# The tail's threshold search counted in steps, its capacity test on ScalarE, its final table of 16 columns

## The chip, the core and the metric

One core of a Trainium2 chip runs the whole program. The metric is the device time of one execution in microseconds (us), the median over several runs. The engines named below are TensorE (PE; its weight loads are listed as PEld), VectorE (DVE), ScalarE (ACT), GpSimd (POOL) and SyncE (SP). Each works through its own instructions in the order of the program; they run beside each other and meet at semaphores.

## What is computed

Three stages follow each other. An attention without softmax makes 12288 rows of 256: `out = u * (relu(z z^T / S)^2 v)`. Then come two layers of eight experts (256 to 1024 to 256). What matters here is how the first layer gives tokens to experts:

```python
logits = x @ w_gate
order = np.argsort(-logits.flatten())
for idx in order:
    tok, e = idx // E, idx % E
    if assigned[tok] >= 0 or counts[e] >= cap:
        continue
    assigned[tok] = e
    counts[e] += 1
```

So the pairs of token and expert are taken from the highest logit down, each expert takes at most `cap` = 1536 tokens, and a token whose expert is full waits for its next best. The second layer routes each token to its best expert and keeps the first 384 of each expert.

## The kernel before

**Order of the stages.** Attention goes over 24 chunks of 512 queries, and the routing of the first layer begins in its shadow. With a threshold `t0`, found from the first three quarters of the tokens (`prep`, L681), every token whose best logit is above `t0` goes to its best expert: the "head". All others, at most 19 x 128, are scattered into a small table in DRAM (`tt`) and are the "tail", together with the last 512 tokens. `tail` (L784) places them.

**The tail's search.** A phase (L833 to L899; nine of them) masks the full experts (LM), takes each remaining token's best logit V and its one-hot TH, and lowers a threshold `hi` as far as no expert gets more than its remaining capacity `kcol`. The threshold is found in three rounds of 32 candidates. A round compares V with the 32 candidates (G, 128 x 23 x 32, L856 or L858), counts per expert with 23 small matmuls (L866, the "capacity test"), compares the counts with `kcol` (gO, L868, VectorE), spreads the result to all partitions with one matmul (L871, the "broadcast") and sums the steps that were not over (gX, L874). After the three rounds NW marks the tokens that are placed (L878), one matmul counts them (L890), and the experts that are full now are masked in the next phase. The size of the next phase's steps is the whole remaining range if a further expert got full, else the finest step (L880 to L887, L839). After the ninth phase the tokens get positions (L904 to L928), and a table of 48 columns, six blocks of 128 places for each of the eight experts, is made by 23 matmuls (L939, `table` at L561, matmul L587). Its columns 4 and 5 of each six are used by the tail.

**Units.** The first layer runs 16 units (`seq`, L1514): eight of width 432, one per expert, for head tokens from the first 40 x 128 places, and then eight of width 256 for tail tokens. A unit has eight blocks f = 0 to 7; a block is six matmuls of layer 1 (L1013), and six of layer 2 (L1163) for the block two before. ScalarE makes the relu hH (L1021) and VectorE the rest hL (L1023). The next weights are loaded by SyncE and split by ScalarE (pH, L220, 128x1024) and VectorE (pL, L225). In blocks 2 to 5 the previous unit's output gets its logits (L1114) and is scattered (L1118); from block 6 on small VectorE steps for the second routing trickle out (L1134 to L1141).

**What sets the order.** `Follow` (L54) puts the steps of `tail` between the matmuls. The program keeps a plan's clock for TensorE, `tp`, and one for VectorE, `td`. At a side point (after each but the last matmul of a group of six, and twice at a block's end) the next step of the tail is issued if `tp` has reached `ready`. Each `yield` of the tail gives costs: a part for TensorE, `pe` (0.25 if not given), one for VectorE, an `extra` and a `lead`:

```python
m.tp += pe
m.dve(d, 0.2)            # td = max(td, tp + 0.2) + d
self.ready = m.td + 0.15 - lead
m.td += extra
```

Other work moves the two clocks too: a matmul adds w/2400 to `tp`, a logit group 0.46 and a turned block of 128 tokens 0.1; hL and the low part of turned tokens add 0.5 to `td`, pL 1.2 (blocks 1, 3, 5, 7), the trickled steps 0.2, 0.35, 0.8 and 0.25, at most one at each of the slow side points (four in a block).

**The forced point.** A unit's gather goes out at block 6 two units before (L1188). Unit 8 needs the tail's table, so its gather waits until block 3 of unit 7, and `late` (L1527) first calls `finish`, which issues all that is left of the tail's steps, one after another.

**Other lines.** `consts` (L135) makes constants early. `row` (L1339) in `ffn2` scales output rows into `orow`; `fin` (L1170) uses `yT` in the first layer. If a check fails, a flag starts `general` (L1473), which does both layers again in a slower way.

Of the kernel before, what the change touches and what calls it, by code (L numbers as in the profile page):

```python
# [53 lines left out]
class Follow:  # L54
# [24 lines left out]
class Moe:  # L79
# [55 lines left out]
    def consts(self, wg1, wg2):  # L135
# [3 lines left out]
        self.idr = c.tile([128, 128], FR, name="idr")  # L139
        nc.scalar.activation(self.idr, self.idf, AF.Copy)  # L140
# [643 lines left out]
    def tail(self, rows):  # L784
# [9 lines left out]
        w3 = c.tile([128, 3], F32, name="w3")  # L794
        for i in range(3):
            nc.vector.memset(w3[:, i:i + 1], float(NTH) ** -i)
# [14 lines left out]
        nc.vector.tensor_scalar(iv, tok[:, :TD], 0.5, -1e36, op0=OP.is_lt, op1=OP.mult)  # L811
# [12 lines left out]
        nc.vector.scalar_tensor_tensor(LT[:, TD:], H[:, :, None].to_broadcast([128, 4, E]), -1e36,  # L824
# [3 lines left out]
        self.diag(k8, kcol)  # L828
        nc.vector.tensor_scalar(cl0, k8, 0.5, 0.0, op0=OP.is_lt, op1=OP.add, accum_out=cc)
        hi = self.t0  # L830
        PH = E + 1
        cl, c2, NW = cl0, cc, None
        for ph in range(PH):  # L833
            LM = R.tile(sh, F32, name="LM")
            nc.vector.scalar_tensor_tensor(LM, cl[:, None, :].to_broadcast(sh), -1e30, LT, op0=OP.mult, op1=OP.add)
            s3 = R.tile([128, 3], F32, name="s3")
            if ph:

                nc.vector.scalar_tensor_tensor(s3, sd[:, 0], d, sd[:, 1], op0=OP.mult, op1=OP.add)  # L839
                cc = c2  # L840
                yield 0.0, 0.5, 0.0, 0.5
            else:
                nc.vector.tensor_scalar(s3, w3, st, None, op0=OP.mult)
            V = R.tile([128, TC], F32, name="tV")
            nc.vector.tensor_reduce(V, LM, AX.X, OP.max)
            M = R.tile([128, NTH], F32, name="gM")
            nc.vector.tensor_scalar(M, self.mrow, s3[:, 0:1], hi, op0=OP.mult, op1=OP.add)
            TH = R.tile(sh, BF, name="tTH")
            nc.vector.tensor_tensor(TH, LM, V[:, :, None].to_broadcast(sh), OP.is_equal)
            yield 0.0, 0.85 if ph else 2.0, 0.0, 0.5  # L850
            for i in range(3):
                G = R.tile([128, TC, NTH], BF, name="gG", tag="gG", bufs=1)
                Vb = V[:, :, None].to_broadcast([128, TC, NTH])
                Mb = M[:, None, :].to_broadcast([128, TC, NTH])
                if i == 0:
                    nc.vector.tensor_tensor(G, Vb, Mb, OP.is_ge)  # L856
                else:
                    nc.vector.scalar_tensor_tensor(G, Vb, sn, Mb, op0=OP.subtract, op1=OP.is_ge)  # L858
                    hi = self.plus(hi, sn)
                if i < 2:  # L860
                    M = R.tile([128, NTH], F32, name="gM")
                    nc.vector.tensor_scalar(M, self.mrow, s3[:, i + 1:i + 2], hi, op0=OP.mult, op1=OP.add)
                yield 0.25, 1.2 if i else 0.9, 0.3
                pc = self.rt()
                for j in range(TC):
                    nc.tensor.matmul(pc[:E, :NTH], TH[:, j, :], G[:, j, :], start=j == 0, stop=j == TC - 1)  # L866
                over = R.tile([E, NTH], BF, name="gO")
                nc.vector.tensor_scalar(over, pc[:E, :NTH], kcol, None, op0=OP.is_gt)  # L868
                yield 0.6, 0.2
                pa = self.rt()  # L870
                nc.tensor.matmul(pa[:, :NTH], self.ones[:E, :], over, start=True, stop=True)  # L871
                x = R.tile([128, NTH], F32, name="gX")
                sn = R.tile([128, 1], F32, name="gn")
                nc.vector.scalar_tensor_tensor(x, pa[:, :NTH], 0.5, s3[:, i:i + 1].to_broadcast([128, NTH]),  # L874
                                               op0=OP.is_lt, op1=OP.mult, accum_out=sn)
            hi = self.plus(hi, sn)
            NW = R.tile(sh, BF, name="tNW")
            nc.vector.scalar_tensor_tensor(NW, V[:, :, None].to_broadcast(sh), hi, TH, op0=OP.is_ge, op1=OP.mult)  # L878
# [727 lines left out]
```

## Time and profile before

| | |
|---|---|
| median of 3 runs | 1636.5 us (1636.49 to 1637.97) |
| profiled execution | 1636.56 us |
| its span, first to last instruction | 1634.8 us |
| mean granted TensorE clock | 0.983 of 2.4 GHz |
| busy: PE, DVE, ACT, POOL | 97%, 73%, 68%, 20% |
| attention, until about | 1106 us |
| first layer, until about | 1460 us |

The profile is of one execution. A matmul's duration covers its way through the array, and matmuls overlap, so the distance of two starts tells what one costs, and a busy share of TensorE is not a share of its peak. The granted clock is 1.00 at 2.4 GHz and 0.50 at 1.2 GHz.

### The profile page before, as it was taken

Reading aid. Unit: us, or ns where it says so; the run is one execution under the profiler, and the core shown is the slowest. Engines: PE = TensorE matmul, PEld = TensorE weight load, DVE = VectorE, ACT = ScalarE, POOL = GpSimd, SP = SyncE. Lnnn points to the kernel's source line nnn. Section 1 sums busy time; section 2 is a strip of 40 time slices with the busy share of each in tenths; the row PEclk is TensorE's granted clock in tenths of the full one; section 3 lists DMA queues with packets and bytes.
Section 4 is the critical chain, followed back from the end, with each engine's and each line's share of the span. In section 5 each row is a group of like instructions: output and inputs, shape, how many; then the busy total and the mean of one; then the engine's idle time right before and its main releaser. Section 6 shows DMA issues by size and latency. Waiting matters only on the chain.

```text
span 1634.8 us, 24914 instructions
## 1 busy us (share of the span) xinstructions
PE 1580.8 (97%) x8570; PEld 1326.7 (81%) x8570; DVE 1186.5 (73%) x2338; ACT 1116.7 (68%) x1937; POOL 333.1 (20%) x518
## 2 busy tenths in 40 slices
PE   8999999999999999999999999999999969989997
PEld 5888887888888888888887777878888759978997
DVE  6877788777778767777877877677777766775652
ACT  7877788777788877778987767884444316644552
POOL 1000000000000000000000478642333113323341
PEclk9999999999999999999999999999999969999999
DMA  6111355322335212224310112223343204644540
GB/s 136 20 27 33 68 136 133 73 70 76 72 67 130 76 46 59 59 66 86 77 33 21 28 20 45 60 80 118 101 124 103 84 19 134 189 134 124 153 129 28
DMA packets 282681, 132.44 MB, mean 81 GB/s; under 512 B 216717, under 2 KB 268173, under 8 KB 282544
## 3 DMA queue, kind: packets, MB, share of 16 engines
q1 hardware_dynamic: 269264, 106.90, 26.0%
q0 software_dynamic: 13280, 23.85, 5.0%
q8 instruction: 69, 1.13, 0.3%
q14 instruction: 68, 0.56, 0.1%
HBM read 84.61 MB, written 40.55 MB: 77 GB/s over the span
## 4 chain that ended last, share of the span: by engine, by line
PE 70%; issue 16%; DVE 7%; POOL 2%; ACT 2%; DMA 1%; SPq 1%; POOLq 0%; DVEq 0%
PE acc L397 12%; PE acc L398 12%; PE acc L399 12%; PE sc L1013 9%; PE sc L368 6%; PE sc L369 6%; PE acc L1163 5%; PE mi L1114 2%; DVE pL L225 1%; PE rt L866 1%; PE mi L336 1%; PE acc L1320 1%; PE acc L1321 1%; PE acc L1322 1%; DVE hL L1023 1%
## 5 line engine op out<-in xcount | busy, mean ns | idle before, releaser
L382 DVE TENSOR_TENSOR aL<-a,aH 128x512 fp32r<-128x512 f32 x576 | 398.6, 693 | 212.9 <-ACT a L377 157.8
L371 ACT ACTIVATE r<-sc 128x512 f32<-128x512 f32 x576 | 343.0, 595 | 186.6 <-PE sc L369 180.7
L397 PE MATMUL acc<-aH,pH 128*128 128x512 f32 x1152 | 449.7, 390 | 0.0
L398 PE MATMUL acc<-aL,pH 128*128 128x512 f32 x1152 | 449.0, 390 | 0.0
L399 PE MATMUL acc<-aH,pL 128*128 128x512 f32 x1152 | 448.5, 389 | 0.0
L379 DVE TENSOR_TENSOR a<-r 128x512 f32<-128x512 f32 x344 | 238.5, 693 | 43.0 <-ACT r L371 41.8
L397 PEld LDWEIGHTS acc<-aH,pH 128*128 128x128 f32 x1152 | 216.7, 188 | 45.6
L399 PEld LDWEIGHTS acc<-aH,pL 128*128 128x128 f32 x1152 | 216.7, 188 | 45.6
L398 PEld LDWEIGHTS acc<-aL,pH 128*128 128x128 f32 x1152 | 216.7, 188 | 45.5
L368 PE MATMUL sc<-zHL 128*128 128x512 f32 x576 | 229.8, 399 | 6.3 <-DVE zHL L280 6.0
L1021 ACT ACTIVATE hH<-sc 128x432 fp32r<-128x432 f32 (+2 forms) x192 | 90.0, 469 | 212.5 <-PE sc L1013 208.2
L369 PE MATMUL sc<-zLH,zHL 128*128 128x512 f32 x576 | 225.3, 391 | 0.2 <-DVE zLH L284 0.2
L380 ACT ACTIVATE aH<-r 128x512 fp32r<-128x512 f32 x344 | 217.8, 633 | 10.9
L347 POOL TENSOR_TENSOR lgs<-lgb 32x128 f32<-32x128 f32 x23 | 15.2, 659 | 853.2 <-DVE lgb L344 853.2
L376 ACT ACTIVATE aH<-r 128x512 fp32r<-128x512 f32 x232 | 146.7, 632 | 7.4
L1023 DVE SCALAR_TENSOR_TENSOR hL<-sc,hH 128x432 fp32r<-128x432 f32 (+2 forms) x192 | 99.3, 523 | 65.6 <-ACT hH L1021 65.4
L377 ACT ACTIVATE a<-r 128x512 f32<-128x512 f32 x232 | 142.8, 616 | 0.0
L368 PEld LDWEIGHTS sc<-zHL 128*128 128x128 f32 x576 | 108.7, 189 | 36.1 <-DVE zHL L280 7.4
L1013 PE MATMUL sc<-xTH,pH 128*128 128x384 f32 (+2 forms) x368 | 125.9, 342 | 5.9 <-DVE hL L1023 5.8
L369 PEld LDWEIGHTS sc<-zLH,zHL 128*128 128x128 f32 x576 | 108.8, 189 | 21.5 <-DVE zLH L284 0.5
L1013 PE MATMUL sc<-xTL,pH 128*128 128x384 f32 (+2 forms) x368 | 120.0, 326 | 0.0
L1013 PE MATMUL sc<-xTH,pL 128*128 128x384 f32 (+2 forms) x368 | 119.8, 326 | 0.0
(333 smaller groups left out, 2261.4 us busy)
## 6 DMA issues: line engine op xcount, KB each, us to landing
raw<-in_moe_w_dram SPq DMA_DIRECT2D x84, 512.0 KB, 3.7
raw<-in_v_dram SPq DMA_DIRECT2D x24, 512.0 KB, 4.3
uraw<-in_u_dram SPq DMA_DIRECT2D x192, 64.0 KB, 2.3
out_dram<-zt SPq DMA_DIRECT2D x24, 512.0 KB, 4.2
xb<-xT SPq DMA_DIRECT2D x14, 512.0 KB, 3.4
zr<-in_z_dram SPq DMA_DIRECT2D x96, 64.0 KB, 2.4
zLH<-zHL POOLq DMA_DIRECT2D x46, 128.0 KB, 2.3
ya<-zt SPq DMA_DIRECT2D x10, 544.0 KB, 3.5
```

What stands on the lines that cost most here:

```text
L368: nc.tensor.matmul(p, lw, zHL[b, c % QC], start=True, stop=False)
L369: nc.tensor.matmul(p, lw, zLH[c], start=False, stop=True)
L371: nc.scalar.activation(r, p, AF.Relu, scale=SCALE)
L376: nc.scalar.activation(HS[s], r, AF.Square)
L377: nc.scalar.activation(a, r, AF.Square)
L379: nc.vector.tensor_tensor(a, r, r, OP.mult)
L380: nc.scalar.activation(HS[s], r, AF.Square)
L382: nc.vector.tensor_tensor(LS[s], a, HS[s].bitcast(F32), OP.subtract)
L397: nc.tensor.matmul(accs[h], vh[sl], HS[s], start=k == 0, stop=False)
L398: nc.tensor.matmul(accs[h], vh[sl], LS[s], start=False, stop=False)
L399: nc.tensor.matmul(accs[h], vl[sl], HS[s], start=False, stop=k == KT - 1)
L1013: nc.tensor.matmul(p, a, b[:, d, :w], start=i == 0, stop=i == 5)
```

## The change

- `Follow`: a yield of five values adds the first to `tp` and sets `ready` to the last after that, without regard to `td`.
- The search counts in steps from the last threshold: U = (V - hi) / st once a phase, compared with fixed rows 1..32, and these times 1/32 and 1/1024 (`m3`); N is the steps taken so far. The per-round rows of thresholds (L847, L862) fall away.
- The capacity test is a relu with the negated capacity as bias, on ScalarE, in place of VectorE's comparison. The step to the next phase is made by three small ScalarE operations and one of VectorE.
- The search's large numbers (1e30 to 1e36) become multiples of the first step, `mk`.
- The place codes (`ti`, `jv`, `pv`), `base`, the early mask and two GpSimd fills move from behind the search to ahead of it. The ninth phase's count and the overflow test move behind the table.
- The table has 2 columns for each expert in place of 6, and `seq` takes columns 2e and 2e + 1. A further check is added after it.
- `consts` loses `idr`, which nothing reads; `row` writes the three rows of a unit into one tile that has the tag of `yT`, of one buffer, in place of three buffers.

The search and the yields (of before, lines with a minus that repeat L834 to L928 are left out; the new code follows in full as far as it has yields):

```diff
                 y = next(self.g)
+                if len(y) == 5 if isinstance(y, tuple) else False:
+
+                    m.tp += y[0]
+                    self.ready = m.tp + y[4]
+                    return
                 pe, d, extra, lead = (y + (0.0, 0.0))[:4] if isinstance(y, tuple) else (0.25, y, 0.0, 0.0)
...
+        w3, m3 = [self.onef[:, :NTH]], [self.mrow]
+        for i in (1, 2):
+            w3.append(c.tile([128, NTH], F32, name="w3%d" % i))
+            m3.append(c.tile([128, NTH], F32, name="m3%d" % i))
+            nc.vector.memset(w3[i], float(NTH) ** -i)
+            nc.vector.tensor_scalar(m3[i], self.mrow, float(NTH) ** -i, None, op0=OP.mult)
         st = R.tile([128, 1], F32, name="st")
         nc.vector.tensor_scalar(st, self.t0, self.lo0, -1.0 / NTH, op0=OP.subtract, op1=OP.mult)
+
+        mk = c.tile([128, 4], F32, name="mk")
+        for i, x in enumerate((-29, 23, 27, -28)):
+            nc.vector.tensor_scalar(mk[:, i:i + 1], st, (1 if x > 0 else -1) * 2.0 ** abs(x), None, op0=OP.mult)
+        lon = c.tile([128, 1], F32, name="lon")
+        nc.vector.tensor_scalar(lon, self.lo0, -1.0 / NTH, None, op0=OP.mult)
...
+        bc = lambda x: x[:, :, None].to_broadcast([128, TC, NTH])
+        for ph in range(PH):
+            LM = R.tile(sh, F32, name="LM", bufs=1)
+            nc.vector.scalar_tensor_tensor(LM, cl[:, None, :].to_broadcast(sh), mk[:, 1:2], LT, op0=OP.mult, op1=OP.add)
+            V = R.tile([128, TC], F32, name="tV")
+            nc.vector.tensor_reduce(V, LM, AX.X, OP.max)
+            if ph:
+                d = R.tile([128, 1], F32, name="std2")
+                nc.vector.tensor_tensor(d, c2, cc, OP.is_gt)
+                st = R.tile([128, 1], F32, name="st")
+                nc.vector.scalar_tensor_tensor(st, dd, d, fine, op0=OP.mult, op1=OP.add)
+                cc = c2
+            U = R.tile([128, TC], F32, name="tU")
+            rs = R.tile([128, 1], F32, name="trs1")
+            nc.vector.reciprocal(rs, st)
+            nc.vector.tensor_scalar(U, V, hi, rs, op0=OP.subtract, op1=OP.mult)
+            N = None
+            for i in range(3):
+                G = R.tile([128, TC, NTH], BF, name="gG", tag="gG", bufs=1)
+                Mb = m3[i][:, None, :].to_broadcast([128, TC, NTH])
+                if i == 0:
+                    nc.vector.tensor_tensor(G, bc(U), Mb, OP.is_le)
+                    TH = R.tile(sh, BF, name="tTH")
+                    nc.vector.tensor_tensor(TH, LM, V[:, :, None].to_broadcast(sh), OP.is_equal)
+                else:
+                    nc.vector.scalar_tensor_tensor(G, bc(U), N, Mb, op0=OP.subtract, op1=OP.is_le)
+                yield 0.25, 1.45 if i else 2.2
+                pc = self.rt()
+                for j in range(TC):
+                    nc.tensor.matmul(pc[:E, :NTH], TH[:, j, :], G[:, j, :], start=j == 0, stop=j == TC - 1)
+                over = R.tile([E, NTH], BF, name="gO")
+                nc.scalar.activation(over, pc[:E, :NTH], AF.Relu, bias=kcol)
+                yield 0.8, 0.0, 0.0, 0.0, 0.45
+                pa = self.rt()
+                nc.tensor.matmul(pa[:, :NTH], self.ones[:E, :], over, start=True, stop=True)
+                x = R.tile([128, NTH], F32, name="gX")
+                sn = R.tile([128, 1], F32, name="gn")
+                nc.vector.scalar_tensor_tensor(x, pa[:, :NTH], 0.5, w3[i], op0=OP.is_lt, op1=OP.mult,
+                                               accum_out=sn)
+                N = self.plus(N, sn) if i else sn
+            NW = R.tile(sh, BF, name="tNW")
+            nc.vector.scalar_tensor_tensor(NW, U[:, :, None].to_broadcast(sh), N, TH, op0=OP.is_le, op1=OP.mult)
+            if ph < PH - 1:
+                h = R.tile([128, 1], F32, name="thi")
+                nc.scalar.activation(h, N, AF.Identity, scale=st, bias=hi)
+                hi = h
+                fine = R.tile([128, 1], F32, name="fine")
+                nc.scalar.activation(fine, st, AF.Copy, scale=float(NTH) ** -3)
+                dd = R.tile([128, 1], F32, name="std")
+                nc.scalar.activation(dd, hi, AF.Abs, scale=1.0 / NTH, bias=lon)
+                nc.vector.scalar_tensor_tensor(dd, dd, -1.0, fine, op0=OP.mult, op1=OP.subtract)
+            nc.vector.scalar_tensor_tensor(LT, NW, mk[:, 0:1], LT, op0=OP.mult, op1=OP.add)
+            if ph == PH - 1:
+                break
+            yield 0.25, 1.1, 0.5
+            pn = self.rt()
+            nc.tensor.matmul(pn[:, :TC * E], self.ones, NW.rearrange("p j g -> p (j g)"), start=True, stop=True)
+            cn = R.tile([128, E], F32, name="tcn")
+            nc.vector.tensor_reduce(cn, pn[:, :TC * E].rearrange("p (j g) -> p g j", g=E), AX.X, OP.add)
+            cl = R.tile([128, E], F32, name="cl")
+            c2 = R.tile([128, 1], F32, name="cc")
+            nc.vector.scalar_tensor_tensor(cl, cn, 0.0, k8, op0=OP.add, op1=OP.is_ge, accum_out=c2)
...
+        yield 0.25, 2.0
...
+        yield 0.3, 1.3
-        yield from self.table(px, s, TC, 6 * E, jv, pv, pool=False)
+        yield from self.table(px, None, TC, 2 * E, jv, pv, pool=False, i=s)
...
-            o = self.f.tile([128, 256], F32, name="orow", bufs=3)
+            if t == 0:
+                O[n] = self.f.tile([128, 2, self.WA], F32, name="orow", tag="yT", bufs=1).rearrange("p a b -> p (a b)")
+            o = O[n][:, t * 256:(t + 1) * 256]
...
-        seq += [(e, [6 * e + 4 + t for t in range(2)], m.WB, m.TB) for e in back]
+        seq += [(e, [2 * e + t for t in range(2)], m.WB, m.TB) for e in back]
```

## Rows read from the trace of the kernel before

**Rows 1.** The page, part 1: busy time, share of span, instructions
```profile
PE 1580.8 (97%) x8570; PEld 1326.7 (81%) x8570; DVE 1186.5 (73%) x2338; ACT 1116.7 (68%) x1937; POOL 333.1 (20%) x518
```
**Rows 2.** Stretches: length, busy PE, PEld, DVE, ACT, POOL, granted clock, DMA share, GB/s
```profile
1112.00:1300.00 188.00, 184.81 (x1390) 156.97 (x1390) 144.43 (x452) 78.04 (x136) 56.01 (x82) 1.00 0.36 111
...
1310.00:1315.00 5.00, 1.55 (x47) 1.43 (x47) 3.75 (x13) 0.00 (x0) 0.00 (x0) 0.50 0.00 2
...
1330.00:1335.00 5.00, 4.94 (x22) 4.19 (x20) 2.89 (x20) 0.53 (x1) 1.00 (x1) 0.50 0.00 0
```
**Rows 3.** Timeline of PE, 1303 to 1337: start, duration (us), engine, line, operation
```profile
1303.12 0.36 PE L1163 MATMUL acc<-hH,pL 128*128 128x432 f32 x1
1303.41 0.73 PE L866 MATMUL rt<-gG,tTH 128*8 128x32 bf16 x23
...
1331.83 0.71 PE L1013 MATMUL sc<-xTH,pH 128*128 128x432 f32 x1
...
1334.13 1.11 PE L1114 MATMUL mi<-sel,yT 128*128 128x136 f32 x4
1334.88 0.72 PE L1163 MATMUL acc<-hH,pH 128*128 128x432 f32 x1
...
1336.89 0.36 PE L1013 MATMUL sc<-xTH,pH 128*128 128x432 f32 x1
```
**Rows 4.** Timeline of POOL at 1334, with idle time before and what ended it
```profile
1333.90 1.00 POOL L969 DMA_INDIRECT g<-xa,tkgb  x1 [29.47 <-DVE b L950]
```
**Rows 5.** The search: lines by source and tile (first and last start); timeline, eighth phase
```profile
L866 PE MATMUL rt<-gG,tTH x621: 176/176/189, 1125.6 to 1317.6; 128*8 128x32 bf16 x156
...
L868 DVE TENSOR_SCALAR gO<-rt,kcol x27: 237/239/240, 1126.3 to 1317.8; 8x32 bf16<-8x32 f32 x27
...
1299.21 0.73 PE L866 MATMUL rt<-gG,tTH 128*8 128x32 bf16 x23
```
**Rows 6.** Timeline of PE, a test and a broadcast between FFN matmuls
```profile
1149.81 0.35 PE L1013 MATMUL sc<-xTL,pH 128*128 128x432 f32 x1
1150.09 0.73 PE L866 MATMUL rt<-gG,tTH 128*8 128x32 bf16 x23
...
1151.05 0.36 PE L1163 MATMUL acc<-hL,pH 128*128 128x432 f32 x1
...
1151.44 0.35 PE L1163 MATMUL acc<-hH,pH 128*128 128x432 f32 x1
1151.72 0.18 PE L871 MATMUL rt<-gO,ones 8*128 8x32 bf16 x1
...
1152.14 0.36 PE L1163 MATMUL acc<-hH,pL 128*128 128x432 f32 x1
```
**Rows 7.** Chain of waits: start, us, the head's table, eight matmuls
```profile
948.23 1.46 PE tabh L587 x8
```
**Rows 8.** Waits, 1108 to 1303: engine, who for, us in total, times, longest
```profile
PEld sc L1013 <- DVE hL L1023: 4.4, 6, 1.4
...
PE sc L1013 <- DVE hL L1023: 2.2, 4, 1.1
...
DVE gO L868 <- PE rt L866: 21.6, 21, 2.9
```
**Rows 9.** ACT by form: first row 1112 to 1300, others the whole span
```profile
L220 ACT ACTIVATE pH<-raw 128x1024 fp32r<-128x1024 f32 x26 | 27.3, 1051 | 0.0
...
L1345 ACT ACTIVATE orow<-acc,gt 128x256 f32<-128x256 f32 x16 | 7.6, 472 | 3.2 <-PE acc L1322 2.2
...
L1306 ACT ACTIVATE ex<-l 128x24 f32<-128x24 f32 x8 | 1.8, 223 | 8.7 <-DVE l L1304 8.6
L279 ACT ACT_TABLE_LOAD x1 | 1.3, 1283 | 0.7 <-PEq L1587 0.7
```
**Rows 10.** Timeline of DVE and PE, a phase's head inside the stop
```profile
1309.06 0.34 DVE L892 TENSOR_REDUCE tcn<-rt 128x8 f32<-128x184 f32 x1
...
1311.80 0.78 PE L866 MATMUL rt<-gG,tTH 128*8 128x32 bf16 x23 [3.33 <-DVE gG L856]
```

More of the change, by code (lines that the diff above doesn't have):

```diff
@@ L921, in tail @@
-        base = R.tile([128, E], F32, name="tbase", bufs=1)
-        nc.vector.tensor_scalar(base, self.hc, float(self.WA), 511.0 - self.WA, op0=OP.max, op1=OP.add)
-        yield 0.7
-        p = self.rt()
-        nc.tensor.matmul(p[:, :E], self.low, tot, start=True, stop=True)
-        nc.vector.tensor_tensor(base, base, p[:, :E], OP.add)
-        nc.vector.tensor_tensor(inc, inc, base[:, :, None].to_broadcast([128, E, TC]), OP.add)
-        s = self.slot_code(inc, oh, TC)
-        yield 1.1
+        NF = self.JF * 128
@@ L937, in tail @@
         nc.vector.tensor_scalar(pv, ti[:, 2], 1.0, None, op0=OP.add)
-        yield 0.4
-        px = self.rt("tabt")
-        yield from self.table(px, s, TC, 6 * E, jv, pv, pool=False)
-        tab = c.tile([128, 2, 6 * E], F32, name="tabB")
-        nc.vector.tensor_tensor(tab.rearrange("p a h -> p (a h)"), px[:, :12 * E],
-                                self.tabH.rearrange("p a h -> p (a h)"), OP.add)
-        self.TB.update(self.tokens(tab[:, 0], tab[:, 1], 6 * E, "b", NF))
-        yield 0.7
+        hi = self.t0
@@ new lines, in tail @@
+        nc.vector.tensor_copy(tot, inc[:, :, TC - 1])
+        yield 0.25, 2.0
+        p = self.rt()
+        nc.tensor.matmul(p[:, :E], self.low, tot, start=True, stop=True)
+        nc.vector.tensor_tensor(base, base, p[:, :E], OP.add)
+        nc.vector.tensor_tensor(inc, inc, base[:, :, None].to_broadcast([128, E, TC]), OP.add)
+        nc.vector.tensor_tensor(inc, inc, oh, OP.mult)
+        s = R.tile([128, TC], I32, name="scs%d" % TC, bufs=1)
+        with nc.allow_low_precision("whole numbers"):
+            nc.vector.tensor_reduce(s, inc.rearrange("p g j -> p j g"), AX.X, OP.add)
@@ new lines, in tail @@
+        yield 0.3, 1.3
+        px = self.rt("tabt")
+        yield from self.table(px, None, TC, 2 * E, jv, pv, pool=False, i=s)
+        tab = c.tile([128, 2, 2 * E], F32, name="tabB")
+        nc.vector.tensor_tensor(tab.rearrange("p a (e h) -> p a e h", h=2),
+                                px[:, :4 * E].rearrange("p (a e h) -> p a e h", a=2, h=2),
+                                self.tabH.rearrange("p a (e h) -> p a e h", h=6)[:, :, :, 4:6], OP.add)
+        self.TB.update(self.tokens(tab[:, 0], tab[:, 1], 2 * E, "b", NF))
@@ new lines, in tail @@
+        yield 0.7
+        FIN = R.tile(sh, BF, name="FIN", bufs=1)
+        nc.vector.tensor_scalar(FIN, LT, mk[:, 3:4], None, op0=OP.is_ge)
+        pn = self.rt()
+        nc.tensor.matmul(pn[:, :TC * E], self.ones, NW.rearrange("p j g -> p (j g)"), start=True, stop=True)
+        cn = R.tile([128, E], F32, name="tcn")
+        nc.vector.tensor_reduce(cn, pn[:, :TC * E].rearrange("p (j g) -> p g j", g=E), AX.X, OP.add)
+        self.over = c.tile([128, E], F32, name="ovr")
+        nc.vector.tensor_tensor(self.over, cn, k8, OP.is_gt)
@@ L1285, in ffn2 @@
         nc, tc, E, NF = self.nc, self.tc, self.E, self.F // 128
[L1286 removed]
+        X, G, GT, ACC, O, scat = {}, {}, {}, {}, {}, []
         T = self.T2
```

121 lines of the change are left out of this document (24 added, 97 removed).

## The prediction

> **What bounds the kernel now.** The page comes first: TensorE is busy for 97% of the span [rows 1]. That is a mean over stages, so the second view is the table of stretches. From 1112 to 1300 us, in the first units of the first expert layer, TensorE has work for 184.8 of 188 us, VectorE for 144, ScalarE for 78. From 1310 to 1315 TensorE has 1.55 us of work in 5, VectorE 3.75, and the granted clock is 0.50, the lower of the two levels (1.2 GHz); it is still 0.50 when work has resumed, from 1330 to 1335 [rows 2]. So one place is not bound by TensorE. The third view, TensorE's own timeline, gives its edges: the last FFN matmul starts at 1303.12, then only the tail's matmuls run, and the next FFN matmul starts at 1331.83 [rows 3]. With 0.20 us for the last one (1151.05 to 1151.44 is two [rows 6]), the stop lasts 28.5 us. After it one block runs at the low clock: six matmuls of layer 1, one logit group (1334.13 to 1334.88), six of layer 2, until 1336.89: 5.1 us [rows 3]. At full clock twelve at 0.20 and the group at no more than its 0.75 are 3.15. The stop's whole price is 28.5 + 1.9 = 30.4 us.
>
> What it waits for: unit 8 is the first that uses tokens of the tail, and its gather is the point (L1188, `late`) where `finish` issues all that is left of the tail with nothing between. The gather goes out at 1333.90, after 29.5 us of idle GpSimd, behind the tail's last VectorE work [rows 4]. The tail's first capacity test had run at 1125.6; the first test of its eighth of nine phases, at 1299.21 [rows 5].
>
> **What the change does to the order.** A tail step goes out when the plan's clock tp reaches `ready`. These are no times but the program's own arithmetic, which sets the order. A phase's yields with nothing else on VectorE (pe + 0.2 + cost + 0.15 - lead for a step dated by VectorE) add up, before, to 0.35 + 0.7 + 1.5 + 1.8 + 1.8, three tests of 1.15, 1.5 and 1.2 = 12.3; after, to 2.8 + 2.05 + 2.05, three tests of 0.8 + 0.45, and 1.7 = 12.35. Alone, the two are equal. But all ten steps of before are dated by td, so each also stands behind whatever hL, pL and one-hot work the plan has queued; of the seven after, the three tests are dated by tp alone. Following the plan through every block puts the first tests of the phases, before, at tp 17.2, 35.7, 56.5, 79.1, 100.4, 122.7, 145.7 and 167.2: 21.4 a phase, so 0.9 of queue a step. The forced point is at 170.5, with the eighth phase's second test next, and that test is what the trace has at 1303.41 [rows 3]. For the change the same arithmetic gives 15.0, 29.4, 43.4, 59.4, 73.8, 90.0, 107.5, 121.6 and 139.5: 15.5 a phase, or 12.35 and four queues of 0.8. The table's last step is at 167.4, in unit 6, block 6; the forced point, unit 7, block 3, is at 180.9 (later, as all of the tail's own pe now counts ahead of it). `finish` then finds nothing to do, with five blocks to spare: **the stop goes whole, 30.4 us.**
>
> **What comes back.** The stop's work has to run between FFN matmuls. From 1149.81 to 1151.05 lie two ordinary intervals and one capacity test: 0.84 for the test. From 1151.44 to 1152.14 lie two and a broadcast: 0.30 [rows 6]. Five of each remained: 4.2 + 1.5. Two counts and the offset matmul: 0.7, at the broadcast's price or less. The table's 23 matmuls, now of 32 columns: at most 23/8 of 1.46 = 4.2, by the head's table of 96 columns [rows 7]; at least one test's 0.84, which also has 23 of 32 columns but weights of 8 columns. The table's weights stay 128 wide, so near the upper: 3.6. Together 10.0, and net so far 30.4 - 10.0 = **20.4 us**. Sixteen columns instead of 48, and the positions prepared ahead, also save VectorE work behind the last phase; hidden under TensorE that is worth nothing more, and without the cover it is part of the 28.5 already counted.
>
> New waits, which the trace only bounds:
> - *ScalarE's test.* The broadcast follows the test by at least three FFN matmuls in the plan (0.45), 0.6 us. The activation takes between 0.22 (128x24, constants only) and 0.47 (128x256, with a pointer); near the small one, 0.3 [rows 9], so the slack is 0.3. ScalarE works in order, and behind the test stands the next hH. Split copies pH of 1.05 fill 27.3 of 188 us, 15% [rows 9]; caught behind one, the mean rest is 0.5, of which some 0.25 passes the slack: 27 x 0.15 x 0.25 = 1.0, and as much for hH, yT and yr: 2.0. Bounds: 0, and 20 if all 27 meet a whole pH (0.75 each). The VectorE form is 0.239 but stands for 21.6 us in line until tests end [rows 5, 8], so the trace favours the move. The Trainium skill ("ScalarE: Activation LUTs", rules for kernel authors) speaks against it: relu belongs on VectorE. By its figure for an activation with a pointer bias (an estimate of 307 ns for 32 elements) the sum stays as it is; by the rule itself the move is a loss.
> - *A phase's head.* From the count's reduction to the first test is 2.74 us, 1309.06 to 1311.80, with nothing else on VectorE [rows 10]. The change drops a threshold row and adds a reciprocal and a rescaling in series: about 3.2. With 0.55 for the count and the wake-up ahead of it, 3.7. The plan allows at least 2.8 units, which are 3.2 us (153.3 units from the first test to the forced point took 177.7 us, 1.16 each), and more than three units at six of eight heads. Eight at 0.3: 2.5. Bounds 0 and 8.
> - *Phase 0*, where eight small operations now stand ahead of the search (each at most a test's 0.24): 1.5. Bounds 0 and 3.
> - *Setup's extra small operations, and unit 8's gather*, which now has two blocks to land: 0.5. Bounds 0 and 2.
> - *A phase's end.* VectorE's step update now waits for three small ScalarE operations in a row, 0.22 each, with the marking of NW as cover. Behind it stand LT and the next hL; TensorE's next tail matmul, the count, needs only NW. It goes into the next term.
> - *The other way.* TensorE waits 4.4 + 2.2 us for hL in this stretch, and VectorE stands 21.6 us in front of tests [rows 8]. That stand goes. Phases are a quarter denser, so I take 2.5 of the 6.6. Bounds: +6.6, and -6 if the density wins.
>
> The identity copy, the markers, the two fills on GpSimd (earlier now, ahead of no gather), and the second layer's rows in one shared tile: nothing; they lie under attention or TensorE, or behind scatters issued a unit earlier. No DMA moves but the gather. Were the shared tile tracked as a whole, the last unit would wait for its own scatters, a few us.
>
> Sum: 20.4 - 2.0 - 2.5 - 1.5 - 0.5 + 2.5 = 16.4. The profiled execution took 1636.56 (span 1634.8 and 1.8 around it) and the median is 1636.50; they agree. 1636.5 - 16.4 = **1620**.
>
> **Rivals.**
> - *Clean hiding.* No new wait shows and most hL waits go: 20.4 + 5 = 25.4, so 1611. For: VectorE's freed stand. Against: heads that need more than the plan allows. Chance 0.13.
> - *A wait at each step.* Heads at 0.6, tests at 0.25: 20.4 - 4.8 - 6.8 - 2 + 2.5 = 9.3, so 1627. For: ScalarE's order, denser phases. Against: ScalarE's 78 of 188 us. Chance 0.17.
> - *Still late.* If the order slipped by more than the five blocks, some 10 us of stop and the low clock would stay: 1636.5 - 18.5 + 7 + 4 = 1629. Against: the same arithmetic hits the present point exactly. Chance 0.03.
> - *Slower: ScalarE's queue ahead of every broadcast.* The broadcast stands in TensorE's in-order stream, so a late activation stops the FFN behind it. It decides once the mean wait over 27 steps passes 16.4/27 + 0.07 = 0.7 us; at 1.05, a whole split copy each time, it is 1620 + 27 x 0.98 = 1646. For: the copies are that long and often follow an hH. Against: their 15%. Table loads for Abs and Identity, 1.28 us each, two a phase, would bring it about; the profile has one load in all, though Copy, Relu, Square and Exp take turns [rows 9]. The Trainium skill (same page, table sets) says that copy, identity, relu and abs are in every set; by it no load is added. No row here shows Abs or Identity. Chance 0.05.
> - *It doesn't do what it says.* If the rescaled search ends elsewhere, the flag sends everything through the general path, both layers again, over 500 us (1112 to 1635): 2140 or more. Chance 0.01.
>
> **How the numbers follow.** Forecast 0.61, by itself 1615 to 1626. A measurement of this kernel can tell about 0.2%, 3.3 us; same is 1633.2 to 1639.8. Faster: the forecast, clean hiding, the waits less 0.02, and late less 0.01: 0.91. Same 0.03, slower 0.06. The range 1611 to 1630 leaves out the lower half of clean hiding (0.06), the upper third of the waits (0.06), half of late, and the slow cases: 0.2.
>
> **What would show it.** Right: no stretch without FFN matmuls in unit 7, granted clock 1.00 from 1112 to the end of unit 15, first tests some 18 us apart (15.5 x 1.16), the table before unit 7, and GpSimd's gather for unit 8 with no tail work ahead of it. By step: about 2 us of broadcasts waiting for ScalarE, about 4 of first tests waiting for VectorE, hL waits down. Wrong: tail matmuls alone between 1300 and 1330; over 10 us of waits for ScalarE's test; a forced gather.

## The result, and the profile after

The change made the kernel slower: 1654.35 us (median of four runs, 1652.22 to 1656.82) against 1637.24 (1636.49 to 1638.07), a ratio of 1.0105, 95% interval 1.0085 to 1.0125: 1% slower. The profiled execution took 1656.35, its span is 1654.2, with a mean granted clock of 0.989. The forecast was 1620, range 1611 to 1630.

The busy line of the page, which answers to [rows 1], shows nothing of it: TensorE at 97% in both.

```profile
PE 1609.1 (97%) x8568; PEld 1324.9 (80%) x8570; DVE 1181.4 (71%) x2266; ACT 1130.4 (68%) x1987; POOL 334.6 (20%) x518
```

TensorE has as many instructions and 28 us more of work, so single instructions became longer. The table of stretches says where. Its columns are those of [rows 2]. First a stretch of attention, before and then after:

```profile
300.00:400.00 100.00, 100.00 (x443) 82.09 (x442) 73.86 (x112) 77.93 (x132) 4.53 (x9) 1.00 0.33 79
```

```profile
300.00:400.00 100.00, 100.00 (x431) 79.68 (x430) 71.25 (x107) 75.36 (x126) 3.03 (x6) 1.00 0.30 71
...
1137.00:1325.00 188.00, 177.76 (x1423) 145.72 (x1421) 146.79 (x431) 85.01 (x176) 52.69 (x76) 0.99 0.32 101
...
1225.00:1230.00 5.00, 4.75 (x36) 3.71 (x37) 4.83 (x20) 1.64 (x3) 0.32 (x3) 0.66 0.46 118
...
1325.00:1345.00 20.00, 19.03 (x118) 16.48 (x117) 15.41 (x60) 7.23 (x13) 4.47 (x9) 1.00 0.30 95
```

In 100 us of attention, with TensorE busy throughout and the clock at 1.00, 431 matmuls start instead of 443. A block of attention is eight matmuls. TensorE's timeline shows the second of one block and the second of the next, eight distances apart, of before:

```profile
329.83 0.39 PE L369 MATMUL sc<-zLH,zHL 128*128 128x512 f32 x1
...
331.64 0.39 PE L369 MATMUL sc<-zLH,zHL 128*128 128x512 f32 x1
```

and of after:

```profile
339.95 0.40 PE L372 MATMUL sc<-zLH,zHL 128*128 128x512 f32 x1
...
341.81 0.40 PE L372 MATMUL sc<-zLH,zHL 128*128 128x512 f32 x1
```

That is 1.81 against 1.86 us for a block. Over 100 to 900 us the mean distance of one 512-column matmul from the next is 227.0 ns before and 233.2 after. Attention has 4608 of them, so the distance makes 28.6 us. Its last one starts at 1106.0 before and at 1137.2 after. I call what is left from there to the end of the span the *rest*: 528.7 us before, 517.0 after. So the rest, in which the tail lies and which the change is about, gained 11.7 us, nearly all of it in the first layer (from attention's last matmul to the layer's last one 352.2 before, 340.1 after), and attention, which it doesn't touch, lost 31.2.

In the rest, the stop of [rows 3] is gone. The table is built in unit 6, between expert matmuls; its timeline and that of GpSimd:

```profile
1328.71 0.45 PE L1186 MATMUL acc<-hH,pH 128*128 128x432 f32 x1
1329.00 0.70 PE L590 MATMUL tabt<-tR,tL 128*128 128x32 bf16 x8
1329.52 0.45 PE L1186 MATMUL acc<-hL,pH 128*128 128x432 f32 x1
...
1354.05 0.99 POOL L992 DMA_INDIRECT g<-xa,tkgb  x1 [0.30 <-issue]
```

Unit 8's first gather (1354.05) waits for nothing but the issue; in [rows 4] it came after 29.47 us behind the tail. The waits from 1137 to 1340, to be read against [rows 8]:

```profile
DVE gX L904 <- PE rt L901: 25.2, 18, 2.5
ACT gO L898 <- PE rt L896: 23.5, 19, 3.3
...
PEld sc L1036 <- DVE hL L1046: 5.3, 5, 1.9
PEld L896 <- DVE tTH L890: 4.9, 5, 1.6
...
PE sc L1036 <- DVE hL L1046: 3.4, 3, 1.5
PE rt L896 <- DVE tTH L890: 3.3, 4, 1.3
PE rt L901 <- ACT gO L898: 0.3, 1, 0.3
```

The stand in front of the tests (21.6 us on VectorE) is now ScalarE's (23.5), and broadcasts wait for it 0.3 us in all. But VectorE still stands 25.2 us in front of the broadcasts' results (gX); before, it had this wait beside that for the tests:

```profile
DVE gX L874 <- PE rt L871: 11.8, 17, 1.9
```

A row of PEld and one of PE can be the same stall, seen by the weight load and by the matmul behind it, as in these two of one wait each:

```profile
PEld sc L1036 <- DVE xTL L1011: 2.3, 1, 2.3
PE sc L1036 <- DVE xTL L1011: 1.9, 1, 1.9
```

So such rows must not be added. What a stall costs is the distance from the start of the last matmul ahead of it (here 1222.95) to the start of the next (1225.25), less an ordinary one (0.20 us, or 0.28 ahead of a test): 2.1 here. Counted so, first tests (L896) cost 3.5 us after the change, 1.4 of it in phase 0 (none before); the waits for hL went from 3.2 to 4.3, and those for xTL, the low part of the turned tokens, from 1.1 to 3.4. The stall at 1225 lies behind a phase's head, through which VectorE works before it comes to xTL, and ahead of the only part of the first layer at the lower clock (0.66 from 1225 to 1230). ScalarE's new operations by form, for [rows 9]:

```profile
L898 ACT ACTIVATE gO<-rt,kcol 8x32 bf16<-8x32 f32 x27 | 7.5, 276 | 23.9 <-PE rt L896 23.5
...
L916 ACT ACTIVATE std<-thi,lon 128x1 f32<-128x1 f32 x8 | 2.4, 295 | 0.0
...
L282 ACT ACT_TABLE_LOAD x1 | 1.3, 1283 | 0.7 <-PEq L1612 0.7
```

A test takes 276 ns (0.3 forecast), and there is still one table load. The Trainium skill ("ScalarE: Activation LUTs", table sets) has copy, identity, relu and abs in every set. This trace agrees.

### The profile page after: what moved, and what is told of

It is laid out like the page before. It is cut to its first block, busy times and chain, and to the rows that moved or that the text cites. A ratio compares the mean times of both kernels' runs of the same rounds, so it can differ in the third digit from the quotient of the medians.

```text
span 1654.2 us, 24878 instructions
## 1 busy us (share of the span) xinstructions
PE 1609.1 (97%) x8568; PEld 1324.9 (80%) x8570; DVE 1181.4 (71%) x2266; ACT 1130.4 (68%) x1987; POOL 334.6 (20%) x518
## 4 chain that ended last, share of the span: by engine, by line
PE 69%; issue 17%; DVE 8%; ACT 2%; POOL 1%; DMA 1%; SPq 1%; POOLq 0%; DVEq 0%; ACTq 0%
PE acc L401 12%; PE acc L400 12%; PE acc L402 12%; PE sc L1036 8%; PE sc L371 6%; PE sc L372 6%; PE acc L1186 4%; DVE pL L228 1%; PE mi L1137 1%; PE mi L339 1%; PE acc L1343 1%; PE acc L1345 1%; PE acc L1344 1%; DVE hL L1046 1%; PE rt L896 1%
## 5 line engine op out<-in xcount | busy, mean ns | idle before, releaser
L385 DVE TENSOR_TENSOR aL<-a,aH 128x512 fp32r<-128x512 f32 x576 | 399.3, 694 | 232.4 <-ACT a L380 185.3
L401 PE MATMUL acc<-aL,pH 128*128 128x512 f32 x1152 | 460.7, 400 | 0.0
L400 PE MATMUL acc<-aH,pH 128*128 128x512 f32 x1152 | 455.9, 396 | 0.0
L371 PE MATMUL sc<-zHL 128*128 128x512 f32 x576 | 233.4, 405 | 7.7 <-DVE zHL L283 6.9
L372 PE MATMUL sc<-zLH,zHL 128*128 128x512 f32 x576 | 229.1, 398 | 0.2 <-DVE zLH L287 0.2
L383 ACT ACTIVATE aH<-r 128x512 fp32r<-128x512 f32 x344 | 217.8, 633 | 10.9
```

The lines of the kernel that those rows point to most:

```text
L371: nc.tensor.matmul(p, lw, zHL[b, c % QC], start=True, stop=False)
L372: nc.tensor.matmul(p, lw, zLH[c], start=False, stop=True)
L383: nc.scalar.activation(HS[s], r, AF.Square)
L385: nc.vector.tensor_tensor(LS[s], a, HS[s].bitcast(F32), OP.subtract)
L400: nc.tensor.matmul(accs[h], vh[sl], HS[s], start=k == 0, stop=False)
L401: nc.tensor.matmul(accs[h], vh[sl], LS[s], start=False, stop=False)
```

## The experiments

**What the code can do to attention.** No instruction of attention differs. But the change drops `idr` (512 bytes), makes the search's and the table's tiles smaller and adds others, and attention's pool lies behind them. By the addresses in the compiled programs attention's tiles start 1184 bytes lower: at 158432 instead of 159616, with V's tiles (the weights `pH`, `pL` of the value part) at 41344 instead of 41856. My first theory was a start off a multiple of 64. Four kernels tried it, three with an unused tile in front of attention's pool (`[128, 8]` for 32 bytes, `[128, 24]` for 96; later `[128, 40]` for 160 and `[128, 104]` for 416) and one with `idr` put back:

```diff
+        pad = R.tile([128, 8], F32, name="pad", bufs=1)
+        nc.gpsimd.memset(pad, 0.0)
         t = R.tile([128, ncol], F32, name="ck0", bufs=1)
```

```diff
         make_identity(nc, self.idf)
+        self.idr = c.tile([128, 128], FR, name="idr")
+        nc.scalar.activation(self.idr, self.idf, AF.Copy)
```

The changed kernel with 32 bytes:

> The changed kernel with one unused tile of 32 bytes per partition more ahead of attention's tiles; nothing else differs, and no instruction of the tail, of attention or of the expert layers changes. Attention's tiles then start at a multiple of 64 bytes again (158464 instead of 158432), as they did in the kernel before (159616). Theory (the placement of attention's moving operands): 512-column matmuls of attention 227 ns apart, as before, instead of 231 to 235; the first expert matmul at about 1106 us instead of 1137.5; the time 1654.4 - 31 = 1623 to 1626, ratio to the kernel before 0.992 to 0.994. Rival (the new code itself, its ScalarE and VectorE work, or the chip): attention stays 31 us longer, 1652 to 1657.

The kernel before with 32 bytes:

> The kernel before with the same unused 32 bytes, which put attention's tiles at 159648, 32 above a multiple of 64. Theory (placement): the matmuls of attention 231 to 235 ns apart, first expert matmul at about 1137 us, the time 1636.5 + 31 = 1666 to 1669, with the stop in unit 7 as before. Rival (the new code): 1636 to 1638, as before.

The changed kernel with 96 bytes:

> The changed kernel with 96 unused bytes instead of 32: attention's tiles at 158528, a multiple of 64 and not of 128 (before: 159616, a multiple of 128). Theory with 64 bytes as the unit: as with 32 unused bytes, 1623 to 1626. Rival with 128 bytes as the unit: attention slow, 1652 to 1657, and the multiple of 64 of the 32-byte variant, which is also one of 128, would not have told them apart.

The changed kernel with `idr`:

> The changed kernel with the rounded copy of the identity put back where it was (512 bytes and one ScalarE copy in the first microseconds). Attention's tiles then start at 158944, still 32 above a multiple of 64, and the tiles of the expert layers and constants lie where the kernel before has them relative to the copy. Theory (placement modulo 64): still slow, 1652 to 1657. Rival (what hurt is that the copy is gone, or the 512-byte move of the constants): about 1624.

Measured: 1668.78, 1677.83, 1678.70 and 1671.98 us, where the kernel before took 1659.5 on this chip. Spacings: 232.5, 232.2, 232.5 and 233.2 ns. So 64 bytes is not it: neither of the two kernels whose start became a multiple of 64 was mended. But the second half of the theory held: 32 unused bytes slow the kernel before as well (432 starts in the stretch that had 443), with none of the new code:

```profile
300.00:400.00 100.00, 100.00 (x432) 79.97 (x431) 71.56 (x107) 75.98 (x128) 4.52 (x9) 1.00 0.31 73
```

**Distance instead of address.** In the kernel before, the addresses of attention's tiles and of V's both leave a remainder of 384 when divided by 512; in the others they don't. The second four, with controls, since this chip's times were not the first one's. One edit,

```diff
+        nc.gpsimd.memset(c.tile([128, 8], F32, name="padc"), 0.0)
         self.idr = c.tile([128, 128], FR, name="idr")
```

moves V's and attention's tiles together (in the kernel before).

The kernel before, unchanged:

> The kernel before, unchanged, with its trace, as the control of this job: the chip of the last job gave 1653 to 1664 for it, against 1636 to 1638 on the first. If the 512-column matmuls' spacing of attention belongs to the kernel and its addresses, it is 227 ns here too, whatever the chip, and a longer time lies in stalls elsewhere (the one of 5 us at 1036 us which the last job's runs show). If it belongs to the chip, the spacing moves with the time: at 1660 it would be 227 + 20/4.6 = 231.

The changed kernel, unchanged:

> The changed kernel, unchanged, as the second control: spacing 231 to 237 ns by either theory, and by the theory of addresses the same figures to the nanosecond as in its first trace (232, 237 and 231 after the three matmuls of attention's value part).

The changed kernel with 160 bytes:

> The changed kernel with 160 unused bytes ahead of attention's tiles, which start at 158592 then: the remainder by 512 is 384, as it is in the kernel before (159616) and in no other kernel tried (224, 256, 320, 416), and as it is for the tiles of V, from which TensorE loads its weights (41344, 384 left). Theory (the spacing depends on where the moving operand lies, modulo 512, alone or against the weights): 227 ns, attention 30 us shorter than the changed kernel's, the time 30 us less than the control's of the changed kernel in this job, some 13 below the kernel before: ratio 0.990 to 0.994. Rival (something else in the new kernel slows attention): spacing 230 to 237, ratio 1.004 to 1.013.

The kernel before, all moved by 32:

> The kernel before with 32 unused bytes among its first constants, so that everything allocated behind them moves by 32 together: V's tiles and attention's tiles both leave 416 by 512. If what counts is the distance of moving operand and weights (a multiple of 512 still), the spacing stays at 227 ns and the time is the control's. If what counts is the moving operand's own address (384 good, 416 bad, as in the variant with 32 bytes ahead of attention's tiles alone), 231 to 234 ns and some 20 us more.

Measured: 1661.70, 1671.73, 1653.69 (ratio 0.9954, 0.9938 to 0.9970) and 1661.36. Spacings: 227.0, 233.2, 227.0 and 227.0. The times of these two chips contain stalls at 1010 to 1070 us in kernels of either kind, like this one of the control, where TensorE waits 7.26 us for a small step of VectorE:

```profile
1010.35 0.39 PE L399 MATMUL acc<-aH,pL 128*128 128x512 f32 x1
1018.00 0.16 PE L500 MATMUL rt<-hM,tri 128*128 128x4 bf16 x1 [7.26 <-DVE cs L495]
```

I did not find their cause, and take from these two jobs only spacings. Those are clear: with the distance of attention's tiles from V's at a multiple of 512 the spacing is 227, whether both leave 384 or both 416, in new code and old:

```profile
300.00:400.00 100.00, 100.00 (x442) 82.11 (x441) 73.86 (x112) 77.92 (x132) 4.54 (x9) 1.00 0.33 79
```

(that is the changed kernel with 160 bytes).

**Which tiles, and which unit.** All further runs were on chips where the kernel before takes 1635 to 1640. On the 160-byte variant single tiles are moved by 32 bytes (and what follows them is put back by 480 more):

```diff
+            if s == 0:
+                nc.gpsimd.memset(W.tile([128, 8], F32, name="pad1", bufs=1), 0.0)
             r = W.tile([128, 512], F32, name="r", bufs=2)
```

(the same ahead of `aH`, and ahead of `zHL`).

Only r and a:

> On the variant with 160 unused bytes (all of attention's tiles at 384 by 512, spacing 227 ns): only r and a, which ScalarE and VectorE write and read and TensorE never touches, move by 32 bytes. If the spacing depends on TensorE's own two reads (moving operand and weights), it stays 227 ns for all eight matmuls of a block. If it comes from the other engines' accesses beside TensorE's, it rises to 230 or more. Where it stays 227, this is also a second run of the 160-byte variant's tail, as control of the next two.

Only aH and aL:

> The same, but only aH and aL, the moving operands of the value part, move by 32 bytes; V's tiles, from which the weights come, and the scores' operands stay. If the distance of moving operand and weights counts, the six value matmuls of a block go to 230 or more (in the kernel before with all of attention's tiles 32 bytes off, 231 to 234) and the two score matmuls stay at 227: some 6 x 576 x 5 ns = 17 us more. If only the scores' or the other engines' accesses count: 227 throughout.

Only zHL and zLH:

> On the 160-byte variant only zHL and zLH move by 32 bytes; they are weights and moving operands of the scores, so within the scores the distance stays 0, while V's weights are loaded beside zLH and the next scores' weights beside aH at a distance of 32. Theory (distance between the streaming operand and the weights loaded meanwhile): two of eight intervals slow, attention 4 to 10 us longer than the variant's 1108 us. Rival (every operand has to lie at one remainder, the scores' too): all or most of them slow, 20 us or more. Rival (only the value part matters): no change.

416 bytes, all of attention:

> The changed kernel with 416 unused bytes: attention's tiles at 128 by 512, V's at 384, a distance of 256. If the unit is 512 bytes: spacing 230 ns or more, about 1650. If it is 256 (distances tried so far: 32, -64, -128, -160 slow, 0 fast): 227 ns and about 1626.

| kernel | moved against V by | time, ratio to before | spacing | last of attention | rest |
|---|---|---|---|---|---|
| r and a | 32 | 1626.71, 0.9929 (0.9909 to 0.9949) | 227.0 | 1107.5 | 517.7 |
| aH and aL | 32 | 1648.82, 1.0064 (1.0041 to 1.0087) | 232.4 | 1132.5 | 516.4 |
| zHL and zLH | 32 | 1641.43, one run | 230.3 | 1121.6 | 518.0 |
| all | 256 | 1625.51, 0.9922 (0.9889 to 0.9955) | 227.0 | 1105.8 | 517.8 |

So what counts is where the tiles lie that TensorE reads; where r and a lie, which only the other engines touch, does nothing. (The other engines write aH, aL, zHL and zLH too; no run parts TensorE's reads of these from the writes.) 256 bytes is the unit as far as tried (distances by 256: 227 ns at 0, and 232 to 233 at 32, 96, 128 and 192); and with that mended the changed kernel takes 1625.5 to 1626.7, 10 to 12 us less than before in the same jobs. My rule for the single matmul fell: with only the scores' tiles moved, not two but five of the eight intervals of a block grew by the median (230 to 235, three stayed at 227), and with only aH and aL moved the interval between the two score matmuls grew most, to 241. The Trainium skill ("TensorE: Matmul & The Clock Gate", step by step) gives TensorE two independent read ports, so that loading the next weights takes nothing from the running matmul. No run here shows the ports. The spacing does depend on how the tiles of the two lie. Whether the rule holds for any stream was tried on the expert layers:

```diff
-            X.append(self.f.tile([128, 2, self.WA], FR, name="xTH"))
+            X.append(self.f.tile([128, 2, self.WA + 16], FR, name="xTH"))
...
-        hH = self.f.tile([128, self.WA], FR, name="hH", bufs=3)[:, :w]
+        hH = self.f.tile([128, self.WA + 16], FR, name="hH", bufs=3)[:, :w]
```

(and xTL, hL; on the variant with the later head, below)

> The variant with 160 unused bytes and the head dated by 3.0, and the moving tiles of the expert layers (xTH, xTL, hH, hL) made 448 columns a half instead of 432, the last 16 unused: 1792 and 3584 bytes, both multiples of 256. They then all lie at 128 by 256, as V's tiles and the weights do; before, at 128, 64, 0 and 192, with the second halves 192 further, and one weight set of three at 0. Theory (a stream at the weights' remainder by 256 runs at 0.443 ns a column, else at 0.455): 432-column matmuls 191 to 192 ns apart instead of 196 to 197, 256-column ones 114 instead of 118; 768 x 5 + 768 x 4 ns = 7 us in the first expert layer, some 2 to 4 more behind it; about 1607 where the variant had 1615.8 and before 1638.4, ratio 0.979 to 0.983. Rival (the rule is one of attention's tiles alone, or of 512 columns): spacing 196 to 197, ratio 0.986.

Measured: 1616.57, ratio 0.9867 (0.9851 to 0.9884), medians of 197 ns for 432 columns and 120 for 256, against 196 and 118. It does not hold there. Why attention's streams have the rule and these don't stays open.

**The tail, part by part.** Four changes to what the prediction priced, three on the 160-byte variant, whose rest is 517.7 and whose first layer is 341.5 (the variant with r and a moved, whose spacing and tail are the same; the 522.7 in an expectation below is from the chip with the stalls). The test on VectorE:

```diff
-                nc.scalar.activation(over, pc[:E, :NTH], AF.Relu, bias=kcol)
+                nc.vector.tensor_scalar(over, pc[:E, :NTH], kcol, 0.0, op0=OP.add, op1=OP.is_gt)
```

> The 160-byte variant with the capacity test on VectorE again (one instruction, same place in the order, same pacing). Theory of the prediction (VectorE is in order and stands in front of each test until TensorE has it done, with the next hL behind): the waits of scores for hL grow from 10.4 + 7.0 us to 14 or more each, the broadcast's waits for the test stay under 4 us, the expert layers take 2 to 6 us longer than the variant's 522.7 from attention's last matmul to the end. Rival (a short test belongs on VectorE: ScalarE's fixed cost and its copies hold the broadcast): 1 to 3 us shorter. The stop in unit 7 does not come back by either.

Measured: 1635.51, ratio 0.9987 (0.9977 to 0.9997); rest 524.6, so 6.9 us more, 8.8 by the medians. Broadcasts now wait for VectorE, and VectorE stands in front of the tests:

```profile
DVE gO L898 <- PE rt L896: 13.9, 17, 1.6
PEld sc L1036 <- DVE hL L1046: 10.5, 11, 1.7
PE sc L1036 <- DVE hL L1046: 7.4, 10, 1.3
PE rt L901 <- DVE gO L898: 5.9, 7, 1.8
```

and the variant's rows for hL:

```profile
PEld sc L1040 <- DVE hL L1050: 12.3, 13, 1.9
PE sc L1040 <- DVE hL L1050: 8.4, 11, 1.6
```

I had expected the waits for hL to grow, and they did not; the broadcast's did, past my bound of 4. By starts the broadcasts cost 6.6 us (0.4 in the variant). Clock was lost too: two such waits, of some 2 us before 1231 and 1262, each precede a part at the lower level, as the mean granted clock of these stretches shows,

```profile
1230.00:1235.00 5.00, 3.88 (x14) 3.52 (x14) 4.47 (x16) 2.19 (x5) 1.03 (x3) 0.71 0.42 142
1260.00:1265.00 5.00, 3.20 (x12) 2.65 (x11) 4.86 (x19) 0.00 (x0) 2.21 (x4) 0.78 0.52 145
```

where the variant has none. Over the first layer the variant loses 3.4 us by parts at the lower clock, this kernel 6.8. The Trainium skill ("ScalarE: Activation LUTs", rules for kernel authors) puts relu on VectorE. Here the move to ScalarE is worth 7 to 9 us, though the instruction is no shorter there (276 ns against 239): what decides is that the broadcast no longer stands behind VectorE's queue. The head of a phase dated later:

```diff
-                yield 0.25, 1.45 if i else 2.2
+                yield 0.25, 1.45 if i else 3.0
```

> The 160-byte variant with a phase's head dated by 3.0 units of VectorE instead of 2.2, so that the first test of a phase goes out about one unit (1.2 us) later. The plan's arithmetic puts the tail's end at 178.4, unit 7, block 3, still ahead of the forced point (180.9). Theory (first tests wait for VectorE because the head is dated too early: 3.3 + 2.0 us in the variant, 4.9 + 3.3 in the changed kernel): these waits fall below 2 us, the expert layers take 2 to 5 us less. Rival (the wait only changes its place: hL comes later, or the last table runs into unit 7's gather): no gain, or a few us lost.

Measured: **1615.77, ratio 0.9860 (0.9844 to 0.9877), rest 509.3**: 8.4 us gained by the rests and 10.9 by the medians, more than I expected, and the best time of this study. The first tests' waits in the variant, and then what is left of them and the waits for hL with the later head:

```profile
PEld L900 <- DVE tTH L894: 5.0, 5, 1.7
PE rt L900 <- DVE tTH L894: 3.3, 4, 1.3
```

```profile
PEld sc L1036 <- DVE hL L1046: 9.1, 13, 1.1
...
PE sc L1036 <- DVE hL L1046: 5.4, 9, 0.7
...
PEld L896 <- DVE tTH L890: 1.0, 2, 0.7
```

Counted by starts over the first layer, first tests cost 0.4 us instead of 3.6 and hL 6.7 instead of 9.9, and no part of it is at the lower clock, where the variant lost 3.4 us. So each is a third of the gain (the first layer takes 332.0 instead of 341.5). The variant's two parts at the lower clock come behind stalls: one behind phase 0's first test at 1124, one behind a wait at 1195 to 1197 for xTL, which stood behind a head's work on VectorE:

```profile
1125.00:1130.00 5.00, 5.00 (x32) 3.92 (x28) 3.88 (x8) 2.29 (x4) 0.83 (x1) 0.66 0.35 105
...
1194.00:1198.00 4.00, 2.05 (x19) 1.35 (x18) 3.86 (x10) 0.54 (x2) 2.50 (x4) 1.00 0.29 82
1198.00:1201.00 3.00, 3.00 (x27) 2.30 (x23) 2.86 (x15) 1.10 (x2) 0.00 (x0) 0.50 0.49 105
```

and the second place with the later head:

```profile
1190.00:1205.00 15.00, 15.00 (x119) 13.15 (x116) 13.03 (x41) 8.36 (x17) 3.86 (x7) 1.00 0.46 130
```

Pacing alone, on the kernel before (with the branch of `step` that a yield of five takes):

```diff
-                yield 0.6, 0.2
+                yield 0.8, 0.0, 0.0, 0.0, 0.45
```

> The kernel before with one thing of the change: the yields behind the capacity tests date the next step by TensorE's clock alone (0.8 and 0.45), not by VectorE's queue. The plan's arithmetic then puts the first tests of the phases at 17, 34, 56, 75, 94, 113, 133, 155, and the forced point at 178.6 with the ninth phase's second test next, instead of the eighth's. Theory of the prediction (fewer dated steps and fewer operations a phase are needed as well): the stop stays, shorter by about one phase, some 17 to 22 us instead of 28.5; the time 5 to 9 us less than before's. Rival (the pacing of the tests was all that was needed): no stop, about 12 us less.

Measured: 1630.94, ratio 0.9960 (0.9932 to 0.9988), rest 522.6, so 4.7 us less by the medians and 6.1 by the rests. The stop stays; the last expert matmul before it starts at 1311.77, the next 17.6 us later, behind the 48-column table at the low clock:

```profile
1311.77 0.36 PE L1167 MATMUL acc<-hH,pL 128*128 128x432 f32 x1
...
1319.34 0.19 PE L929 MATMUL rt<-ttot,low 128*128 128x8 bf16 x1 [2.26 <-DVE ttot L924]
1325.04 4.66 PE L591 MATMUL tabt<-tR,tL 128*128 128x96 bf16 x23 [5.51 <-DVE tL L586]
1329.40 0.71 PE L1017 MATMUL sc<-xTH,pH 128*128 128x432 f32 x1
```

So pacing takes 11 us off the stop of 28.5. For what is left the rest of the change is needed; which part of it (fewer steps in a phase, the positions prepared ahead, the narrow table) no run tells apart. The table at 48 columns:

```diff
-        yield from self.table(px, None, TC, 2 * E, jv, pv, pool=False, i=s)
+        yield from self.table(px, None, TC, 6 * E, jv, pv, pool=False, i=s)
```

> The 160-byte variant with the final table built at 48 columns again (the upper 32 stay empty), everything else as changed. VectorE builds three times as many one-hots, in three groups of eight, and 23 matmuls have 96 columns for 32. By the plan's arithmetic the tail still ends a block ahead of unit 7 (171.3 against 180.9). Theory: the matmuls cost 23/8 of 1.46 - 0.70 = 2.2 us more and the one-hots lie beside other work: 2 to 4 us more than the variant's expert layers. Rival (the width is worth much, since VectorE holds hL back): 6 us or more, or the stop comes back.

Measured: 1629.93, ratio 0.9950 (0.9913 to 0.9987), rest 523.2: 5.5 us more than the variant, between the two expectations. By the medians it is 4.4 against the 416-byte variant of the same job, and the intervals of the two ratios overlap. Eight of its matmuls take 1.62 us instead of 0.70,

```profile
1304.21 1.62 PE L590 MATMUL tabt<-tR,tL 128*128 128x96 bf16 x8
```

which is 2.6 for 23, and a stretch at 1315 to 1325 is at 0.81 and 0.85 of the clock, which is 1.7:

```profile
1315.00:1320.00 5.00, 3.03 (x12) 2.84 (x12) 3.71 (x16) 0.84 (x2) 0.00 (x0) 0.81 0.33 108
1320.00:1325.00 5.00, 5.00 (x26) 4.55 (x24) 0.61 (x1) 1.62 (x4) 1.08 (x2) 0.85 0.01 2
```

## Why the prediction was wrong, step by step

- **The step that failed** is "The identity copy, the markers, the two fills on GpSimd …, and the second layer's rows in one shared tile: nothing; they lie under attention or TensorE". It priced what instructions do, and neither it nor any other term asks where the tiles behind them go. The change moved attention's tiles against V's by 672 bytes (1184 - 512), no multiple of 256, and attention took 31.2 us more, 28.6 of it by the distance of its matmuls. The copy itself is cleared: its 512 bytes move both alike, and putting it back left the spacing at 233.2. The 672 come from the search and the table: by the addresses the pool with their tiles went from 30348 to 29644 bytes, and another one got 32 more. No rival had this, and the slower side of the range had no mechanism of this kind. Shown by the 160- and 416-byte variants (the spacing returns) and by the 32 bytes in the kernel before (it goes).
- **The stop** (30.4 us) was right: gone whole, the table in unit 6, the gather free, first tests 18.8 us apart (1154.4 to 1304.4, eight phases; 18 forecast), and the clock at 1.00 but for the part at 1225. With the tiles put back the time is 1625.5 to 1626.7, inside the range and 6 above the 1620.
- **The table** was mis-sized: 0.70 + 0.70 + 0.65 = 2.1 us for 23 matmuls, not 3.6; and its width was worth some 4 to 5.5, where the prediction gave it nothing beyond the stop.
- **ScalarE's test**: 0.3, not 2.0. ScalarE did not hold the broadcasts, and the rival in which it does lost its ground.
- **Heads and phase 0**: 1.4 for phase 0 and 2.1 for the other heads, 3.5 in all; 1.5 and 2.5 were forecast. The term was right.
- **The other way** was misread and had the wrong sign. Its "4.4 + 2.2 us" are one set of stalls in two rows; by starts they cost 3.2 before. After, they cost 4.3: 1.1 lost, not 2.5 gained. "That stand goes" holds only in part, as VectorE now stands 25.2 us in front of broadcasts; that and the denser phases are the likely reason, which no run shows by itself.
- **Not in the sum**: the waits for xTL, 2.3 us more, and the part at the lower clock behind the longest of them (0.66 from 1225 to 1230, so 0.34 x 5 = 1.7).

With these the sum is 16.4 + 1.5 + 1.7 + 0.5 - 3.6 - 2.3 - 1.7 = 12.5, where the rest shows 11.7. The 0.8 between them is less than single runs of the changed kernel differ by (1652.2 to 1656.8).

## What to carry to other kernels

A change that adds, drops or resizes a tile moves what is allocated behind it; before trusting a comparison, see whether the spacing of matmuls that were not edited is the same, and if not, pad the pool. For 512-column fp32 streams of the kind here, keep the streaming tiles and the weights at one remainder by 256 bytes. A late result can cost TensorE twice, by the wait and by a lower clock behind it, so date a step for when its result is really ready: 0.8 in a plan's cost was worth 8 to 11 us. And don't add the waits of PEld and PE: they can be the same stall.

## What the runs showed that was not expected

- Spacing of 512-column matmuls by where tiles lie: 227.0 ns at a distance of 0 modulo 256 bytes, 232.2 to 233.2 for all of attention off it, 230.3 and 232.4 for parts of it, the same on every chip seen.
- Expert matmuls of 432 and 256 columns show no such effect (196 or 197, and 118 to 120 ns).
- Some stalls of TensorE were followed by a stretch at half clock, as from 1198 to 1201 above, and others were not: phase 0's first test waited as long after the change (at 1154) as in the variant (at 1124), and only the variant's clock fell.
